# Attention and two MLPs on one core: a product of two weights handed to the scheduler earlier, and a row scaling moved from POOL to ScalarE

## The chip, the cores and the metric

The kernel runs on one core of one Trainium2 chip. The metric is the device time of one execution in microseconds (us). Three runs of the kernel before gave 1234.72, 1235.17 and 1236.8 us; their median is 1235.17 us.

## The reference

Attention over 4 batches of 12 heads, 448 positions, head size 64, feeds two MLPs over the 1792 rows that it makes. All in float32 precision.

```python
q_n, k_n = rmsnorm(q, g_q), rmsnorm(k, g_k)
scores = scale * np.matmul(q_n, k_n.transpose(0, 1, 3, 2))
attn = np.exp(scores - np.max(scores, axis=-1, keepdims=True))
attn = attn / (np.sum(attn, axis=-1, keepdims=True) + 1e-09)
x = np.matmul(attn, v)            # laid out as 1792 x 768
h = x @ w_in                      # 768 -> 2048
x = np.maximum(0.01 * h, h) @ w_out
a, b = x @ w1, x @ w2             # 768 -> 1024 each
out = ((a * b) @ w3) @ w_last     # w_last is moe2_w_out
```

## The kernel before

Every float32 product is made of three matmuls of rounded parts: a tile x is split into `xh` (rounded) and `xl` (the rest), and likewise a weight into `wh` and `wl`; the three are wh·xh, wh·xl and wl·xh (`group`, L491). Since nothing stands between w3 and w_last, the kernel multiplies these two weights with each other first: `combine_weights` (L511) makes w3·w_last, 1024 x 768, in 384 matmuls into the tile `pw`, each 128 x 384, and stores the result in DRAM (`wc`). The two weights arrive as 64-bit words; each piece is loaded (L402), turned into float32 (`to_float32`: POOL L420, ScalarE L422 and L425, VectorE L427 and L431) and split (`split`: ScalarE L456, VectorE L184). The eight pieces of w_last are kept in `lasth` and `lastl` for the whole product, the sixteen of w3 go through `wh` and `wl`.

The attention works on pairs of heads. A pair takes two **slots**, one for each half of its query rows, so that there are 48 slots. A slot's work is: the score matmuls `ps` (L123, 12 of them), the scaling with the row's minimum (VectorE L254), the exponential with its row sum (ScalarE L263), 1 / sum (VectorE L268, L269), and the multiplication of the four 112 x 448 tiles `p` by it (POOL, L272). Two slots later TensorE transposes them (`pt`, L286), VectorE and ScalarE copy the transposes to `pth` (L103, L101), and a matmul with v gives the pair's values (`po`, L123). The preparation of later pairs (square sums L148 and L149, keys L204 to L219) lies between.

Two generators are interleaved in `fill` (L978): the attention's steps, and a stream of MLP matmuls handed out in proportion to the steps done. From slot `COMBINE_SLOTS[0]` to slot `COMBINE_SLOTS[1]` the stream is `combine_weights`; then, up to slot 26, it is the first two of four parts of the first MLP for batch 0 (`early`, its matmuls in the tile `ps_mm`); after slot 26 it is all the rest for batches 0 and 1 (`late`). The parts of the weights that `early` made are kept in DRAM and loaded again by SyncE (SP) for `late` (L443). This order of the program, with the priorities of L43, goes to a scheduler that writes each engine's final order. So a number in `COMBINE_SLOTS` changes the order on every engine. After slot 47 the last two batches run through the MLPs alone.

The lines that matter below are L40 (the two slots), L272 (the multiplication), L978 to L995 (`fill`), L1023 to L1027 (its calls).

Of the kernel before, what the change touches and what calls it, by code (L numbers as in the profile page):

```python
# [11 lines left out]
AF = mybir.ActivationFunctionType  # L12
ALU = mybir.AluOpType
# [23 lines left out]
KEYS_AHEAD = 1  # L37
P_TILES = 8
TOGETHER = 2000
COMBINE_SLOTS = 5, 17  # L40
EARLY = 2
PRIORITY = dict(
    values=200, p_transpose=600, scores=600, prep=600, load=100, statistics=100, keys=50  # L43
# [4 lines left out]
def attention_then_moe(  # L48
# [22 lines left out]
    nc = tc.nc  # L71
# [17 lines left out]
    def bank(name):  # L89
        return psum.tile([P, 512], F32, tag="ps", name=name)  # L90
# [24 lines left out]
    def together(matmuls):  # L115

        one = None
        for out, a, x, begin, end in matmuls:
            with ExitStack() as behind:
                if one is not None:  # L120
                    behind.enter_context(tc.high_priority(TOGETHER))
                    behind.enter_context(tc.issue_after(one.ins))
                one = nc.tensor.matmul(out, a, x, start=begin, stop=end)  # L123
        return one
# [100 lines left out]
    def scores(t, half):  # L225

        if t >= NH // 2:
            return
        x = pairs[t]
        pair = heads[2 * t : 2 * t + 2]  # L230
        if half == 0:
            x["sums"] = small.tile([CP, 2, NCH], F32, tag="sum", name="sum")
            for h in pair:
                h["p"] = [None] * NCH
        ps = [[bank("ps")[:CP, :S] for _ in range(2)] for _ in range(2)]
        chunks = range(2 * half, 2 * half + 2)
        terms = [("qh", "kh"), ("ql", "kh"), ("qh", "kl")]
        x["scored"] = together(
            (
                ps[c % 2][e],  # L240
                x[q][mine(e), c * CP : (c + 1) * CP],
                x[k][mine(e)],
                n == 0,
                n == len(terms) - 1,
            )
            for c in chunks
            for n, (q, k) in enumerate(terms)
            for e in range(2)
        )
        for c in chunks:  # L250
            for e, h in enumerate(pair):
                p = h["p"][c] = att.tile([CP, S], F32, tag="p", name="p", bufs=P_TILES)
                low = small.tile([CP, 1], F32, tag="low", name="low", bufs=8)
                nc.vector.tensor_scalar(  # L254
                    p,
                    ps[c % 2][e],
                    x["scale"][:, e, c : c + 1],
                    None,
                    op0=ALU.mult,
                    op1=ALU.min,  # L260
                    accum_out=low,
                )
                exps[t] = nc.scalar.activation(  # L263
                    p, p, AF.Exp, bias=low, scale=-1.0, accum_out=x["sums"][:, e, c : c + 1]
                )

        r = small.tile([CP, 2, 2], F32, tag="r", name="r")
        nc.vector.tensor_scalar_add(r, x["sums"][:, :, 2 * half : 2 * half + 2], 1e-9)  # L268
        nc.vector.reciprocal(r, r)  # L269
        for c in chunks:  # L270
            for e, h in enumerate(pair):
                nc.gpsimd.tensor_scalar(  # L272
                    h["p"][c], h["p"][c], r[:, e, c % 2 : c % 2 + 1], 1.0, op0=ALU.mult, op1=ALU.mult
                )

    def mine(i):
        return slice(D * (i % 2), D * (i % 2 + 1))
# [64 lines left out]
    def attention_steps():  # L342

        for t in range(NH // 2 + 2):
            ranked(values, t - 2)
            yield 2 * t
            for half in range(2):
                s = 2 * t + half
                for kc in range(NCH):
                    ranked(p_transpose, s - 2, kc)  # L350
                    yield s
                ranked(scores, t, half)
                for _ in range(NCH):
                    yield s
                if half:
                    ranked(keys, t + KEYS_AHEAD)
                    ranked(load, t + 2)
                    ranked(statistics, t + STATS_AHEAD)
                else:
                    load_v(2 * t)  # L360
                    ranked(prep, t + 1)
                    load_rows(t + STATS_AHEAD)
                run_later()
                yield s
# [610 lines left out]
    per_slot = 2 * NCH + 2  # L975
    slots = COMBINE_SLOTS

# [99 lines left out]
```

## Time and profile before

| | |
|---|---|
| median of three runs | 1235.17 us |
| the profiled execution's own time | 1229.4 us |
| its span, first to last instruction | 1227.6 us |
| TensorE (PE) matmuls busy | 1157.6 us, 94% |
| VectorE (DVE) busy | 777.9 us, 63% |
| ScalarE (ACT) busy | 662.7 us, 54% |
| GpSimd (POOL) busy | 390.2 us, 32% |
| mean granted TensorE clock | 0.967 of full |

Busy shares are means over stretches with different limits. The attention with its stream of MLP work takes the first 810 us; in the last 418 us POOL does nothing. A wait is put down to the releaser that came last, and the chain of waits is followed back from the last instruction. "Granted clock" is the share of the full TensorE clock: 1.00 is 2.4 GHz and 0.50 is 1.2 GHz, and a value between is a mean over both.

### The profile page before, as it was taken

The numbers are of one execution on the slowest core, as the hardware profiler recorded it, in microseconds if no ns is written. First come the engines' busy times: TensorE is split into PE (matmuls) and PEld (weight loads), VectorE is DVE, ScalarE is ACT, GpSimd is POOL, SyncE is SP. The second block draws the span as 40 slices with busy tenths as digits, with TensorE's granted clock in tenths as the row PEclk, the third lists the DMA queues.
The fourth block names the chain that finished last, engine by engine and source line by source line (L and its number), as shares of the span: only waits on it lengthen the run. The fifth ranks groups of instructions, "written<-read, shape, count | busy, mean of one in ns | idle before, by whom it ended". The sixth has DMA issues, their size and how long they took to land.

```text
span 1227.6 us, 17006 instructions
## 1 busy us (share of the span) xinstructions
PE 1157.6 (94%) x6096; PEld 966.4 (79%) x6096; DVE 777.9 (63%) x1511; ACT 662.7 (54%) x1343; POOL 390.2 (32%) x474
## 2 busy tenths in 40 slices
PE   2779999998979999999999999999999999899998
PEld 1456778776668788888878888888999999699997
DVE  7997777889852375857854465276346455954553
ACT  7676667777644475666654664245443334533431
POOL 3654345677731344367642443200000000000000
PEclk8669999998889999999999999999999999999999
DMA  8433335877576534534421441062212021112202
GB/s 256 143 99 108 113 123 199 303 257 262 186 298 193 172 119 157 165 126 165 166 88 64 152 161 53 34 227 64 77 35 78 26 77 59 58 39 67 72 35 99
DMA packets 65381, 158.93 MB, mean 129 GB/s; under 512 B 7440, under 2 KB 32784, under 8 KB 65296
## 3 DMA queue, kind: packets, MB, share of 16 engines
q1 hardware_dynamic: 45648, 73.94, 19.0%
q10 hardware_dynamic: 10944, 49.29, 12.0%
q0 software_dynamic: 8704, 34.61, 7.5%
q8 instruction: 48, 0.79, 0.3%
q14 instruction: 37, 0.30, 0.1%
HBM read 114.95 MB, written 42.86 MB: 129 GB/s over the span
## 4 chain that ended last, share of the span: by engine, by line
PE 64%; DVE 7%; DMA 4%; ACT 1%; issue 1%; POOL 1%; SPq 0%; ACTq 0%; DVEq 0%; POOLq 0%
PE ps_mm L499 26%; PE ps_o L499 13%; PE ps_b L499 9%; PE ps_c L499 5%; PE po L123 3%; PE pt L286 3%; PE ps L123 3%; PE ps_a L499 2%; DVE ol L184 1%; DVE wl L184 1%; DMA wh<-kept_first_mlp_h 1%; DMA qk_sb<-qk 1%; DMA x_f<-xd 1%; DMA w<-w_out 1%; DVE acc L863 1%
## 5 line engine op out<-in xcount | busy, mean ns | idle before, releaser
L272 POOL TENSOR_SCALAR p<-p,r 112x448 f32<-112x448 f32 x192 | 150.9, 802 | 63.4 <-DVE r L269 34.4
L184 DVE TENSOR_TENSOR wl<-raw,wh 128x512 fp32r<-128x512 f32 (+1 forms) x136 | 113.9, 839 | 74.9 <-ACT wh L705 35.1
L499 PE MATMUL ps_mm<-xh,wh 128*128 128x448 f32 x384 | 143.0, 373 | 7.3 <-DMA wh<-kept_first_mlp_h 7.0
L263 ACT ACTIVATE p<-p,low 112x448 f32<-112x448 f32 x192 | 126.5, 661 | 40.4 <-DVE p L254 40.1
L499 PE MATMUL ps_mm<-xl,wh 128*128 128x448 f32 x384 | 146.8, 382 | 0.0
L499 PE MATMUL ps_mm<-xh,wl 128*128 128x448 f32 x384 | 141.9, 370 | 0.1
L254 DVE TENSOR_SCALAR_CACHE_REDUCE p<-ps,rs 112x448 f32<-112x448 f32 x192 | 122.0, 678 | 27.7 <-PE ps L123 27.7
L286 PE MATMUL pt<-ident,p 112*112 112x112 f32 x768 | 107.2, 278 | 25.7 <-POOL p L272 20.7
L286 PEld LDWEIGHTS pt<-ident,p 112*112 112x112 f32 x768 | 87.5, 143 | 52.8 <-POOL p L272 26.6
L499 PE MATMUL ps_mm<-gl,wh 128*128 128x448 f32 x288 | 109.5, 380 | 0.0
L427 DVE SCALAR_TENSOR_TENSOR raw<-w,raw 128x768 uint32<-128x768 uint32 (+1 forms) x80 | 76.0, 949 | 51.1 <-ACT w L425 50.9
L499 PE MATMUL ps_mm<-gh,wl 128*128 128x448 f32 x288 | 106.2, 369 | 0.9 <-DMA wl<-kept_first_mlp_l 0.9
L499 PE MATMUL ps_mm<-gh,wh 128*128 128x448 f32 x288 | 106.3, 372 | 0.6 <-DMA wh<-kept_first_mlp_h 0.6
L499 PE MATMUL ps_o<-gl,wh 128*128 128x448 f32 x288 | 104.1, 365 | 0.0
L499 PE MATMUL ps_o<-gh,wl 128*128 128x448 f32 x288 | 100.5, 365 | 0.0
L499 PE MATMUL ps_o<-gh,wh 128*128 128x448 f32 x288 | 99.1, 365 | 0.0
L420 POOL TENSOR_SCALAR raw<-w 128x768 f32<-128x768 f32 (+1 forms) x80 | 70.2, 878 | 84.3 <-DVE wl L184 51.9
L422 ACT ACTIVATE w<-w 128x768 uint32<-128x768 uint32 (+1 forms) x80 | 63.5, 794 | 47.0 <-DMA w<-w_out 16.1
L425 ACT ACTIVATE w<-w 128x768 f32<-128x768 f32 (+1 forms) x80 | 63.1, 789 | 45.6 <-POOL raw L420 45.6
L499 PEld LDWEIGHTS ps_mm<-xh,wh 128*128 128x128 f32 x384 | 73.0, 190 | 15.5 <-DVE y L155 6.3
L123 PE MATMUL po<-pth,v_sb 112*64 112x448 f32 x384 | 80.7, 562 | 1.9 <-ACT pth L101 1.1
L499 PEld LDWEIGHTS ps_mm<-xl,wh 128*128 128x128 f32 x384 | 73.2, 191 | 10.8 <-issue 4.9
(136 smaller groups left out, 2650.8 us busy)
## 6 DMA issues: line engine op xcount, KB each, us to landing
w<-w_in ACTq DMA_DIRECT2D x16, 768.0 KB, 4.8
w<-w_out ACTq DMA_DIRECT2D x24, 512.0 KB, 3.8
w<-w ACTq DMA_DIRECT2D x16, 768.0 KB, 4.5
qk_sb<-qk SPq DMA_DIRECT2D x48, 224.0 KB, 4.2
w<-w3t ACTq DMA_DIRECT2D x16, 512.0 KB, 3.3
kept_first_mlp<-raw POOLq DMA_DIRECT2D x16, 384.0 KB, 4.7
kept_first_mlp<-raw POOLq DMA_DIRECT2D x24, 256.0 KB, 3.5
kept_second_mlp<-raw POOLq DMA_DIRECT2D x16, 384.0 KB, 3.0
```

The costliest lines, as they stand in the source:

```text
L123: one = nc.tensor.matmul(out, a, x, start=begin, stop=end)
L184: e.tensor_tensor(out, x, y.bitcast(F32), op=ALU.subtract)
L254: nc.vector.tensor_scalar(p, ps[c % 2][e], x["scale"][:, e, c : c + 1], None, op0=ALU.mult, op1=ALU.min, accum_out=low,)
L263: exps[t] = nc.scalar.activation(p, p, AF.Exp, bias=low, scale=-1.0, accum_out=x["sums"][:, e, c : c + 1])
L272: nc.gpsimd.tensor_scalar(h["p"][c], h["p"][c], r[:, e, c % 2 : c % 2 + 1], 1.0, op0=ALU.mult, op1=ALU.mult)
L286: nc.tensor.transpose(pt[:, c * CP : (c + 1) * CP], h["p"][c][:, kc * CP : (kc + 1) * CP], ident[:CP, :CP],)
L420: nc.gpsimd.tensor_scalar(out, h, 0.0, 1.0, op0=ALU.mult, op1=ALU.mult)
L422: nc.scalar.activation(low, low, AF.Copy, scale=2.0**-29)
L425: nc.scalar.activation(h, h, AF.Copy, scale=2.0**-112)
L427: nc.vector.scalar_tensor_tensor(top, high, 3, top, op0=ALU.logical_shift_left, op1=ALU.bitwise_or)
L499: nc.tensor.matmul(ps[:, :n], a, x, start=begin, stop=end, skip_group_check=on)
L863: nc.vector.tensor_tensor(acc[m, b], ps[:, :S], acc[m, b], op=ALU.add)
```

## The change

`COMBINE_SLOTS` goes from 5, 17 to 1, 14: the product of w3 and w_last is handed out from slot 1 to slot 14 and no longer from slot 5 to slot 17, and the early part of the first MLP from slot 14 and no longer from slot 17, up to slot 26 as before. And ScalarE multiplies the tiles `p` by 1 / sum, with an activation `Copy` whose scale is a column of `r`; before, POOL did. No operation is added or left out.

```diff
-COMBINE_SLOTS = 5, 17
+COMBINE_SLOTS = 1, 14
...
         for c in chunks:
             for e, h in enumerate(pair):
-                nc.gpsimd.tensor_scalar(
-                    h["p"][c], h["p"][c], r[:, e, c % 2 : c % 2 + 1], 1.0, op0=ALU.mult, op1=ALU.mult
+                nc.scalar.activation(
+                    h["p"][c], h["p"][c], AF.Copy, scale=r[:, e, c % 2 : c % 2 + 1]
                 )
```

The built programs show what the scheduler makes of it, at three places. The first is TensorE between the score matmuls of slot 2 and those of slot 3 (`pt` are the transposes of slots 0 and 1, `pw` the product of the two weights). Before:

```order
L123 MATMUL ps<-kl,qh 112x448 x2
L286 MATMUL pt<-ident,p 112x112 x28
L123 MATMUL ps<-kh,qh 112x448 x2
L123 MATMUL ps<-kh,ql 112x448 x2
L123 MATMUL ps<-kl,qh 112x448 x2
```

With the change:

```order
L123 MATMUL ps<-kl,qh 112x448 x2
L286 MATMUL pt<-ident,p 112x112 x28
L499 MATMUL pw<-lasth,wh 128x384
L499 MATMUL pw<-lastl,wh 128x384
L499 MATMUL pw<-lasth,wl 128x384
```

Twelve `pw` matmuls now stand ahead of slot 3's scores; before, the first `pw` stood behind slot 6's. Counted over the whole order: ahead of the first score matmul of slot 8 there were 31 `pw` and now are 115; ahead of slot 16's there were 289 `pw` and no `ps_mm`, and now are all 384 `pw` and 64 `ps_mm`, with eight `pt` fewer; ahead of slot 28's both orders have the same matmuls, and from there on they are alike.

The second place is ScalarE behind the exponentials of slots 0 and 1 (`w` is a weight on its way to float32, `r` is 1 / sum). Before:

```order
L456 ACTIVATE lasth<-raw 128x768
L402 DMA w_862<-w_last 128x1536
L148 ACTIVATE sq<-qk_sb 112x512
L148 ACTIVATE qk_sb<-qk_sb 112x512
L425 ACTIVATE w_754<-w_754 128x512
L153 ACTIVATE y<-ss 112x16
L456 ACTIVATE lasth<-raw 128x768
```

With the change:

```order
L456 ACTIVATE lasth<-raw 128x768
L402 DMA w_487<-w_last 128x1536
L148 ACTIVATE qk_sb<-qk_sb 112x512
L272 ACTIVATE p<-p,r 112x448 x4
L148 ACTIVATE sq<-qk_sb 112x512
L456 ACTIVATE lasth<-raw 128x768
L402 DMA w_534<-w_last 128x1536
L422 ACTIVATE w_487<-w_487 128x768
L153 ACTIVATE y<-ss 112x16
L272 ACTIVATE p<-p,r 112x448 x4
L456 ACTIVATE wh<-raw 128x512
```

The eight multiplications of slots 0 and 1 now stand among the conversions of w_last. Ahead of ScalarE's first exponential of slot 8 there are now 32 multiplications, four more pieces of w3 (twelve activations of 128 x 512) and five more copies of `pw` (L534) than before; between there and slot 16's another 32 multiplications, and ten more activations of weights and one copy of `pw` fewer than before.

The third place is SP where `late` begins, at slot 26: the loads of the kept weight parts. Before:

```order
L443 DMA wh<-kept_first_mlp_0_h 128x768
L167 DMA qt_sb<-qt 128x448
L178 DMA v_sb<-v 112x2x256
L443 DMA wh<-kept_first_mlp_1_h 128x768
L443 DMA wl<-kept_first_mlp_0_l 128x768
L443 DMA wl<-kept_first_mlp_1_l 128x768
```

With the change:

```order
L443 DMA wh<-kept_first_mlp_0_h 128x768
L443 DMA wl<-kept_first_mlp_0_l 128x768
L178 DMA v_sb<-v 112x2x256
L134 DMA qk_sb<-qk 112x2x256 x2
L167 DMA qt_sb<-qt 128x448
L443 DMA wh<-kept_first_mlp_1_h 128x768
L443 DMA wl<-kept_first_mlp_1_l 128x768
```

On TensorE the same place, with the tiles' numbers (3960 and 3961 are the parts of weight 0, 3970 is one of weight 1), read before:

```order
L286 MATMUL pt_4010<-ident_81,p_3853 112x112
L499 MATMUL ps_mm_3982<-xl_2218,wh_3960 128x448
L499 MATMUL ps_mm_4025<-xh_2217,wh_3970 128x448
L286 MATMUL pt_4037<-ident_81,p_3693 112x112
L286 MATMUL pt_4037<-ident_81,p_3701 112x112
```

and now reads:

```order
L286 MATMUL pt_4010<-ident_81,p_3734 112x112
L499 MATMUL ps_mm_3982<-xl_2503,wh_3960 128x448
L499 MATMUL ps_mm_3982<-xh_2502,wl_3961 128x448
L499 MATMUL ps_mm_3982<-xh_2502,wh_3960 128x448
L499 MATMUL ps_mm_3982<-xl_2503,wh_3960 128x448
```

Before, the first matmul that needs weight 1 stood third, ahead of the transposes, of slot 26's scores and of nearly all the products of weight 0; now 18 products of weight 0 come ahead of it, and both parts of weight 0 are loaded ahead of weight 1.

## Rows read from the trace of the kernel before

**Rows 1.** Busy time by stretches cut at slots 0, 8, 16, 28: engines' busy, clock, DMA.

```profile
core 0: us, PE busy (x) PEld busy (x) DVE busy (x) ACT busy (x) POOL busy (x), PEclk, DMA share, GB/s
14.00:104.00 90.00, 63.36 (x300) 40.63 (x300) 78.40 (x173) 67.11 (x146) 50.18 (x50) 0.72 0.44 141
104.00:199.00 95.00, 93.53 (x567) 71.27 (x566) 75.34 (x178) 67.12 (x159) 43.91 (x58) 1.00 0.40 128
199.00:290.00 91.00, 89.92 (x506) 68.84 (x506) 74.63 (x138) 66.26 (x139) 62.52 (x85) 1.00 0.78 273
290.00:360.00 70.00, 56.52 (x287) 42.49 (x286) 57.38 (x115) 43.31 (x96) 42.16 (x59) 0.83 0.68 252
...
399.00:810.00 411.00, 407.50 (x2264) 341.10 (x2263) 240.04 (x477) 231.00 (x472) 177.41 (x202) 1.00 0.38 127
```

**Rows 2.** Waits of PE over the span: total us, times, longest.

```profile
PE pt L286 <- POOL p L272: 20.7, 8, 10.4
...
PE ps_mm L499 <- DMA wh<-kept_first_mlp_h: 7.6, 3, 6.1
```

**Rows 3.** PE's timeline, matmuls of pw: start us, us.

```profile
90.48 0.52 PE L499 MATMUL pw<-lastl,wh 128*128 128x384 f32 x1
90.80 0.52 PE L499 MATMUL pw<-lasth,wl 128*128 128x384 f32 x1
...
101.22 0.34 PE L499 MATMUL pw<-lasth,wh 128*128 128x384 f32 x1
101.39 0.34 PE L499 MATMUL pw<-lastl,wh 128*128 128x384 f32 x1
```

**Rows 4.** The chain that ended last: start us, us, what.

```profile
707.37 7.49 PE ps_mm L499 x36
...
790.60 1.53 PE pt L286 x16
```

**Rows 5.** ACT's timeline, an exponential and the reading of its sum.

```profile
22.97 0.66 ACT L263 ACTIVATE p<-p,low 112x448 f32<-112x448 f32 x1
23.53 0.19 ACT L263 ACTIVATION_READ_ACCUMULATOR p<-p,low 112x1 f32 x1
```

**Rows 6.** ACT by form, 14 to 104 us: busy us, mean ns, idle before.

```profile
L422 ACT ACTIVATE w<-w 128x512 uint32<-128x512 uint32 x7 | 4.7, 668 | 0.1
L425 ACT ACTIVATE w<-w 128x512 f32<-128x512 f32 x6 | 4.1, 677 | 2.1 <-POOL raw L420 2.1
...
L456 ACT ACTIVATE wh<-raw 128x512 fp32r<-128x512 f32 x4 | 2.5, 620 | 0.0
```

**Rows 7.** ACT by form, 0 to 350 us.

```profile
L534 ACT ACTIVATE wo<-pw 128x384 f32<-128x384 f32 x16 | 7.6, 478 | 2.8 <-PE pw L499 2.8
```

**Rows 8.** Waits of ACT, 14 to 104 us, the two longest.

```profile
ACT w L425 <- POOL raw L420: 6.2, 4, 4.1
ACT sq L148 <- DMA qk_sb<-qk: 6.2, 2, 3.6
```

**Rows 9.** Timelines of DVE and POOL, 19 to 38 us.

```profile
19.26 0.94 DVE L427 SCALAR_TENSOR_TENSOR raw<-w,raw 128x768 uint32<-128x768 uint32 x1
...
30.32 1.28 DVE L427 SCALAR_TENSOR_TENSOR raw<-w,raw 128x768 uint32<-128x768 uint32 x1
...
37.51 1.15 DVE L150 TENSOR_SCALAR ss<-ss 112x16 f32<-112x16 f32 x1
...
30.14 8.49 POOL L272 TENSOR_SCALAR p<-p,r 112x448 f32<-112x448 f32 x8
```

**Rows 10.** PE's timeline where `late` begins.

```profile
345.91 0.45 PE L499 MATMUL ps_mm<-xl,wh 128*128 128x448 f32 x1
352.43 0.71 PE L499 MATMUL ps_mm<-xh,wh 128*128 128x448 f32 x1 [6.08 <-DMA wh<-kept_first_mlp_h]
```

**Rows 11.** SP's timeline of DMA issues at the same place.

```profile
340.95 0.33 SPq L443 DMA_DIRECT2D wh<-kept_first_mlp_h  x1
...
345.38 0.82 SPq L443 DMA_DIRECT2D wl<-kept_first_mlp_l  x2
```

**Rows 12.** Busy time in a stretch ahead of the first pw.

```profile
80.00:90.00 10.00, 9.13 (x41) 6.14 (x39) 9.61 (x25) 4.89 (x13) 6.49 (x7) 0.50 0.01 3
```

## Prediction

> **What bounds the kernel now.** I cut the span where slots 0, 8, 16 and 28 begin on PE and read each stretch for the engine that is never free. From 399 us on PE is busy 407.5 of 411 us at the full clock [rows 1], and the orders are alike from there: nothing can be won. So the question is when slot 28 begins, at 399 us before. From 104 to 290 us PE is full too, 93.5 of 95 and 89.9 of 91 us. PE time is lost in two places. In 14 to 104 us PE is busy 63.4 of 90 us at a mean clock of 0.72 (a mix of 1.2 and 2.4 GHz), which is at most 63.4 x 0.72 = 46 us of work at full speed; DVE is busy 78.4 there, so it is nearly full, ACT 67.1, POOL 50.2. The longest wait that PE has for another compute engine is here, 20.7 us in eight pieces for the multiplication on POOL [rows 2]. In 290 to 360 us PE is busy 56.5 of 70 us at 0.83, about 47 us of work: 23 us are lost, 6.1 of them in one wait for a kept weight [rows 2, 10].
>
> **The change, term by term**, each as a shift of the beginning of slot 28.
>
> *PE work moved forward.* Ahead of slot 8 there are 84 more `pw`. At the full clock they start 0.17 us apart [rows 3]: 84 x 0.175 = 14.7 us. Ahead of slot 16 it is 95 `pw` (16.6 us), 64 `ps_mm` at 7.49 / 36 = 0.208 us (13.3 us), less eight transposes at 1.53 / 16 = 0.1 us (0.8 us) [rows 3, 4]: 29.1 us. So slots 0 to 7 get 14.7 us of PE work more, slots 8 to 15 get 14.4 more, and slots 16 to 27 get 29.1 less.
>
> *Slots 0 to 7.* What does this cost where PE had room? No row shows the new activation. From below it can cost what an exponential of the same tile occupies, since the exponential does a pointer operand and more: it starts 0.56 us before the reading of its sum [rows 5]; from above its whole 0.66 us. I take 0.56, because ACT's instructions overlap like these two. ACT gets 32 of them, 17.9 us; four pieces of w3, 4 x (0.668 + 0.677 + 0.620) = 7.9 us, less about 0.1 us overlap each, 6.7; five copies of `pw`, 5 x 0.38 = 1.9 [rows 6, 7]. That is 26.5 us on an engine that was busy 67.1 of 90: 93.6 us, 3.6 more than the stretch has. DVE gets thirteen operations of the w3 pieces, at two thirds of the 0.94 us of 128 x 768 [rows 9] 8 us: 86.6 of 90, also nearly full. So ACT becomes the bound. At best it never waits, and slot 8 begins 3.6 us later; at worst it keeps all its 22.9 us of idle time, and slot 8 begins 26.5 us later. Some waits go with the multiplication on POOL (6.2 us were for POOL's part of a conversion), some do not (6.2 us for `qk_sb` to land) [rows 8]. I let 5.4 us stay, nearer to the low end because the scheduler put other ready work between: **+9 us**.
>
> A row bears on DVE's side. The same 128 x 768 operation took 0.94 us with POOL idle and 1.28 us beside POOL's eight multiplications (8.49 us from 30.14), and a 112 x 16 operation took 1.15 us there [rows 9]. The multiplications leave POOL, so DVE should get some of this back: 0.34 us of the first and at most the whole of the second, 1.5 us for two slots and 6 us for eight. The Trainium skill, GPSIMD Engine Reference, section Specifications, says that POOL's SBUF interfaces are shared with VectorE, with contention for DVE's two-port modes and two-input instructions; the trace agrees. By that sentence all of it would come back, and the term would be nearer +5 than +9; I keep +9, since ACT and not DVE is last here.
>
> *Slots 8 to 15.* PE was full and stays so: 93.5 + 14.4 = 108 us at the least, **+14.4**. ACT: 67.1, 17.9 for 32 multiplications and about 7 for ten weight activations (between 6 and 9, by their columns from rows 6) come to 92 of 109 us, which fits.
>
> *Slots 16 to 27.* PE has **-29.1**. ACT: 66.3 + 43.3 in the 161 us up to 360 [rows 1], 48 x 0.56 = 27 more, less the 16 that went forward (8.6 and 7): 121 us, which fits.
>
> *The loss around 290 to 360 us.* Before, PE stopped for 6.08 us at weight 1 [rows 10], whose load was issued at 340.95, before `wl` of weight 0, at 345.38 [rows 11]. Now 18 products of weight 0 (18 x 0.208 = 3.7 us) stand ahead of weight 1, and both parts of weight 0 are loaded first; the half clock behind the stop goes too. Against this, weight 1 now stands behind a load of `qk_sb` on SP. The ends are nothing (the stall finds another place) and 23 us (all of the loss). I take **-8**: this stop and 2 us of its half clock. The rest hangs on loads of 64-bit weights that are now spread over more slots, which I do not count.
>
> *From slot 28 on.* ACT gets 80 x 0.56 = 45 us: 231 + 45 = 276 of 411 us. PE covers it. What it costs if a copy out of PSUM comes late behind a multiplication: between 0 and 10 us; **+2**.
>
> Sum: 9 + 14.4 - 29.1 - 8 + 2 = **-11.7 us**. Against the profiled execution's 1229.4 us that is 1217.7; that execution is 5.8 us under the median of the runs, so on the median's scale I forecast **1223 us**.
>
> **Rivals.**
>
> *ACT's queue holds everything up (slower).* ACT works in order, and a multiplication waits for `r` from DVE; behind it stand exponentials, conversions and copies out of PSUM that PE waits for. If ACT keeps all its idle time in slots 0 to 7, the first term is +26.5: 26.5 + 14.4 - 29.1 - 8 + 2 = +6, 1241 us. If it keeps it in slots 8 to 15 too (27.9 us, so 120 where PE needs 109) it is another 11: 1252. It decides from 17 of 22.9 us kept, where the sum passes zero. For it: both ACT and DVE are then full, and their waits are on each other. Against: eight places where PE waited for POOL are gone.
>
> *The early product wakes the clock and the later loss goes (faster).* In 80 to 90 us PE was busy 9.13 of 10 at the 1.2 GHz level [rows 12]; `pw` starts 0.32 us apart at 90 us and 0.17 at 101 us, after eleven microseconds of nearly unbroken matmuls [rows 3]. With `pw` from slot 3 on, PE is denser sooner. If ACT also waits for nothing (+3.6) and the loss at 290 to 360 us goes altogether (-23): 3.6 + 14.4 - 29.1 - 23 + 2 = -32, 1203; half of that way, -22, 1213. The Trainium skill, TensorE: Matmul & The Clock Gate, Part 1, says that the clock is throttled by default and that activity releases it; the trace has both levels as it says. Without such a release the 84 `pw` cost 84 x 0.32 = 27 us of PE in slots 0 to 7, which with 63.4 makes 90 of 99 us and still fits, so that the clock alone does not decide.
>
> *The loads set the pace (no change).* From 199 to 360 us the DMA engines are busy 0.78 and 0.68 of the time at 273 and 252 GB/s [rows 1]. If slot 28 waits for the kept weights and not for PE, the work moved forward only makes room to wait in: 1235 us. Against it: PE was full up to 290 us under the same load.
>
> That the change does not do what it says is not among them: the order shows both parts.
>
> **How the numbers follow.** Less than 0.2% (2.5 us) is about what a measurement of this kernel cannot tell from no change. The forecast, between -4 and -18 us: 0.45. The faster rival, beyond -18: 0.21. The loads: 0.12. The slower rival, from +3: 0.22. So faster 0.66, same 0.12, slower 0.22. For eight in ten I leave out half of what lies beyond -30 and what lies beyond +8, a tenth each: 1206 to 1243 us. The likeliest case by itself is 1217 to 1231.
>
> **What would show it.** In the profile of the changed kernel: slot 8's first score matmul at about 113 us and slot 16's at about 222 (before 104 and 199), yet slot 28's at about 385; ACT busy over 90 of the 99 us of slots 0 to 7; no wait of `pt` for POOL, and short ones for ACT in its place; no stop of 6 us at the first kept weights; PE still over 99% busy after slot 28. I am wrong if slot 8 begins after 125 us (the queue of ACT), if a loss of 20 us stays between slots 16 and 28 (the loads), or if PE's idle time after slot 28 grows by more than 10 us.

## The result, and the profile after

The changed kernel takes 1217.32 us (median of four runs, 1213.81 to 1222.62) against 1235.38 us (1234.72 to 1236.8) for the kernel before in the same comparison. The ratio is 0.9856, with a 95% interval of 0.9828 to 0.9884: 17.8 us or 1.4% faster. The forecast was 1223 us, the range 1206 to 1243. The profiled execution took 1215.56 us, with a span of 1213.8 us and a mean granted clock of 0.975 (before 1229.4, 1227.6 and 0.967). So the two profiles are 13.8 us apart and not 17.8: the kernel before was profiled in an execution 6 us under its median, the change in one 1.8 us under its own, and some 4 us of the gain stand in none of the stages below.

First the busy time of the engines in stretches cut where slots 0, 8, 16, 22 and 28 now begin, with one more cut at 343 us. The columns are those of [rows 1].

```profile
14.00:115.00 101.00, 72.23 (x380) 51.43 (x380) 82.76 (x182) 89.93 (x190) 26.53 (x25) 0.80 0.50 156
115.00:227.00 112.00, 108.56 (x639) 86.41 (x638) 82.19 (x181) 92.95 (x204) 36.41 (x49) 0.97 0.56 184
227.00:294.00 67.00, 63.27 (x357) 44.86 (x357) 59.35 (x128) 63.72 (x143) 31.37 (x46) 0.97 0.79 273
294.00:343.00 49.00, 47.81 (x280) 34.70 (x280) 44.20 (x99) 46.25 (x102) 19.35 (x27) 1.00 0.69 248
343.00:382.00 39.00, 39.00 (x219) 32.86 (x216) 12.51 (x38) 21.88 (x50) 5.57 (x5) 1.00 0.63 202
382.00:794.00 412.00, 410.21 (x2266) 343.39 (x2266) 235.20 (x477) 274.52 (x552) 115.19 (x122) 1.00 0.38 127
```

Slot 28 begins at 382 us where it began at 399. Slots 0 to 7 and 8 to 15 have become longer, 101 and 112 us against 90 and 95. The gain is the third to fifth row together: 155 us where slots 16 to 27 took 200. From 294 us on PE has hardly a gap and the full clock, where in 290 to 360 us before it was busy 56.5 of 70 us at 0.83 [rows 1].

The same in one table for the two kernels and five of the runs below. A stage begins with the first score matmul of its first slot on PE. A cell has the length of the stage in us, then in brackets what PE lost in it: the time in which no matmul ran, and half of the busy time in stretches at the 1.2 GHz level.

| kernel | slots 0 to 7 | 8 to 15 | 16 to 21 | 22 to 27 | 28 to the end |
|---|---|---|---|---|---|
| before | 89.2 (26.0, 18.6) | 95.0 (1.5, 0) | 86.0 (0.9, 0) | 114.0 (13.6, 8.1) | 828.8 (14.3, 1.7) |
| the change | 100.4 (28.4, 13.2) | 111.9 (3.4, 3.4) | 67.6 (3.7, 1.7) | 88.1 (1.2, 0) | 831.4 (13.5, 5.1) |
| e1, slots alone | 96.4 (27.9, 9.3) | 106.3 (0.9, 0) | 73.3 (9.3, 1.7) | 92.0 (2.0, 0) | 836.3 (16.7, 8.1) |
| e2, ScalarE alone | 91.6 (31.7, 12.8) | 95.0 (1.4, 1.7) | 86.7 (2.2, 1.7) | 105.8 (9.9, 4.6) | 830.9 (15.3, 1.7) |
| e10, POOL's time put back | 102.6 (32.0, 10.9) | 105.8 (0, 0) | 73.6 (8.9, 3.7) | 97.7 (5.2, 5.1) | 835.3 (16.9, 5.0) |
| e14, from slot 0 | 100.6 (23.1, 6.5) | 100.2 (0, 0) | 66.4 (4.3, 0) | 93.9 (3.1, 3.3) | 834.1 (15.1, 6.5) |
| e15, POOL's time, no wait | 120.4 (38.8, 20.1) | 114.7 (4.7, 1.7) | 68.0 (2.9, 3.4) | 91.5 (2.0, 3.4) | 834.1 (16.7, 4.0) |

What is left of a stage when its losses are taken off is PE's work at full speed. It went from 44.6 to 58.8 us in slots 0 to 7, from 93.5 to 105.1 in slots 8 to 15, and from 85.1 + 92.3 to 62.2 + 86.9 in slots 16 to 27: 25.8 us forward by the first two, 28.3 by the last. The last column differs by some us between profiles of kernels with one order there (before 828.8, e6 832.3), so 2 or 3 us in it say nothing. A row is one execution: e1's, 1219.86 us, is the fastest of its six (median 1225.71), so its row shows e1 some 6 us too short.

The waits of PE after, total us, times, longest:

```profile
PE pt L286 <- ACT p L272: 18.5, 4, 14.7
PE pk L209 <- DVE y L155: 12.6, 1, 12.6
...
PE ps_mm L499 <- DMA wl<-kept_first_mlp_l: 1.1, 1, 1.1
...
PE ps_mm L499 <- DMA wh<-kept_first_mlp_h: 0.6, 1, 0.6
```

The wait of the transposes for the multiplication has changed its releaser, and its total little (20.7 us for POOL [rows 2]); its longest piece has grown from 10.4 to 14.7 us. The wait for kept weights has gone from 7.6 us for `wh` [rows 2] and 0.9 for `wl` to 1.7 for both parts. SP's timeline where `late` begins (start us, us, DMA issue):

```profile
327.20 0.35 SPq L443 DMA_DIRECT2D wh<-kept_first_mlp_h  x1
328.38 0.34 SPq L443 DMA_DIRECT2D wl<-kept_first_mlp_l  x1
332.05 0.33 SPq L178 DMA_DIRECT2D v_sb<-v  x1
332.48 0.97 SPq L134 DMA_DIRECT2D qk_sb<-qk  x2
335.34 0.35 SPq L167 DMA_DIRECT2D qt_sb<-qt  x1
335.86 0.35 SPq L443 DMA_DIRECT2D wh<-kept_first_mlp_h  x1
```

Both parts of weight 0 are asked for by 328.4 us, 14 us ahead of slot 26 (342.7). The `wh` of weight 1, issued at 340.95 before [rows 11], goes out at 335.86.

What the multiplication costs on ACT: its group over the span (busy us, mean ns, idle before), (192 of them, 113 us in all):

```profile
L272 ACT ACTIVATE p<-p,r 112x448 f32<-112x448 f32 x192 | 113.0, 672 | 11.1 <-DVE r L269 10.8
```

And a piece of ACT's timeline (start us, us):

```profile
33.54 1.85 ACT L272 ACTIVATE p<-p,r 112x448 f32<-112x448 f32 x3
35.02 0.33 ACTq L402 DMA_DIRECT2D w<-w_last  x1
35.22 0.73 ACT L272 ACTIVATE p<-p,r 112x448 f32<-112x448 f32 x1
```

One lasts 0.67 us, and three of them take (35.22 - 33.54) / 3 = 0.56 us of ACT each, the price that the prediction took from an exponential [rows 5].

### The profile page after: what moved, and what is told of

Its sections match the earlier page's. It is cut to its first block, busy times and chain, and to the rows that moved or that the text cites. A ratio compares the mean times of both kernels' runs of the same rounds, so it can differ in the third digit from the quotient of the medians.

```text
span 1213.8 us, 16887 instructions
## 1 busy us (share of the span) xinstructions
PE 1150.1 (95%) x6096; PEld 964.3 (79%) x6096; DVE 759.7 (63%) x1511; ACT 761.7 (63%) x1535; POOL 238.2 (20%) x282
## 4 chain that ended last, share of the span: by engine, by line
PE 63%; ACT 13%; DVE 8%; DMA 7%; issue 4%; POOL 1%; ACTq 0%; SPq 0%; DVEq 0%; POOLq 0%
PE ps_mm L499 24%; PE ps_o L499 13%; PE ps_b L499 9%; PE ps_c L499 5%; ACT p L272 3%; PE po L123 3%; PE pt L286 3%; ACT p L263 3%; PE ps L123 3%; PE ps_a L499 2%; DMA w<-w_out 2%; ACT w L425 1%; DVE ol L184 1%; DMA w<-w_in 1%; DMA w<-w3t 1%
## 5 line engine op out<-in xcount | busy, mean ns | idle before, releaser
L286 PE MATMUL pt<-ident,p 112*112 112x112 f32 x768 | 100.7, 266 | 26.2 <-ACT p L272 18.5
L286 PEld LDWEIGHTS pt<-ident,p 112*112 112x112 f32 x768 | 82.6, 135 | 51.3 <-ACT p L272 21.1
L272 ACT ACTIVATE p<-p,r 112x448 f32<-112x448 f32 x192 | 113.0, 672 | 11.1 <-DVE r L269 10.8
L427 DVE SCALAR_TENSOR_TENSOR raw<-w,raw 128x768 uint32<-128x768 uint32 (+1 forms) x80 | 69.2, 867 | 55.8 <-ACT w L425 55.4
L420 POOL TENSOR_SCALAR raw<-w 128x768 f32<-128x768 f32 (+1 forms) x80 | 69.5, 869 | 166.5 <-DVE wl L184 105.8
L499 PE MATMUL ps_o<-gh,wl 128*128 128x448 f32 x288 | 100.6, 366 | 0.0
L705 ACT ACTIVATE wh<-raw 128x512 fp32r<-128x512 f32 (+1 forms) x52 | 36.3, 698 | 77.3 <-PE ps_b L499 34.5
L456 ACT ACTIVATE wh<-raw 128x512 fp32r<-128x512 f32 (+1 forms) x84 | 59.8, 714 | 33.4 <-PE ps_mm L499 33.4
```

What stands on the lines that cost most here:

```text
L272: nc.scalar.activation(h["p"][c], h["p"][c], AF.Copy, scale=r[:, e, c % 2 : c % 2 + 1])
L286: nc.tensor.transpose(pt[:, c * CP : (c + 1) * CP], h["p"][c][:, kc * CP : (kc + 1) * CP], ident[:CP, :CP],)
L420: nc.gpsimd.tensor_scalar(out, h, 0.0, 1.0, op0=ALU.mult, op1=ALU.mult)
L427: nc.vector.scalar_tensor_tensor(top, high, 3, top, op0=ALU.logical_shift_left, op1=ALU.bitwise_or)
L456: self.rounded = nc.scalar.activation(flat[0], x, AF.Copy)
L499: nc.tensor.matmul(ps[:, :n], a, x, start=begin, stop=end, skip_group_check=on)
```

## The experiments

Each has the change or the kernel before as its base. Times are medians, ratios are to the kernel before on the same chip with their 95% intervals.

**e1: the slots alone.** The kernel before with the new slots; POOL multiplies.

```diff
-COMBINE_SLOTS = 5, 17
+COMBINE_SLOTS = 1, 14
```

> Only the slots change (1, 14); POOL still multiplies. Theory A (PE work moved forward pays, ACT's extra work costs): the same work stands ahead as in the change (115 pw ahead of slot 8, 384 pw and 55 ps_mm ahead of slot 16), without ACT's 18 us in slots 0 to 7, so the gain is like that of the change or larger: 1210 to 1222 us. Theory B (the multiplication's move carries the gain, since p is ready sooner and DVE is free of POOL): within 4 us of before, 1231 to 1239, and slot 28 begins near 399 us.

Measured: 1225.71 us (1219.86 to 1228.88), ratio 0.9903 (0.9876 to 0.9929).

**e2: the multiplication alone.** The change with the old slots.

```diff
-COMBINE_SLOTS = 1, 14
+COMBINE_SLOTS = 5, 17
```

> Only the multiplication moves to ScalarE; the slots stay at 5, 17. Theory A: 13 pw more stand ahead of slot 8 and 10 ahead of slot 16, ACT gets 18 us more in slots 0 to 7, slot 28 begins within 6 us of 399 and the time is 1230 to 1240 us. Theory B: 1213 to 1225 us, and slot 8 begins before 104 us.

Measured: 1228.2 us (1224.83 to 1231.63), ratio 0.9931 (0.9906 to 0.9956). Both times lie between what the two theories expected: each part gains by itself, 1.0% and 0.7%, and together they give 1.4%, somewhat less than the sum. So the multiplication on ScalarE is, over the whole kernel, no price paid for the slots. It gains some 8 us where the prediction gave it only costs. In e2 slot 8 begins at 105.6 us, 1.8 later than before, so none of that is gained ahead of slot 8. By the table, e1's loss is smaller than that of the kernel before in slots 22 to 27 (2.0 us for 21.7) and larger in 16 to 21 (11.0 for 0.9); e2 keeps most of the loss in 22 to 27 (14.5).

**e3 and e4: one end of the slots each**, in the change.

```diff
-COMBINE_SLOTS = 1, 14
+COMBINE_SLOTS = 1, 17
```

> The changed kernel with the slots 1, 17: the product begins early, the first MLP late as before (89 pw ahead of slot 8, 309 ahead of slot 16, no ps_mm there). Theory A (work moved into PE's idle time of slots 0 to 7 pays): most of the slots' gain is here, 1218 to 1223 us. Theory C (the earlier start of the first MLP pays, since its weights are loaded and converted earlier and PE's loss in slots 22 to 27 goes): no gain over the multiplication alone, 1226 to 1232 us, with 10 us or more lost in slots 22 to 27.

```diff
-COMBINE_SLOTS = 1, 14
+COMBINE_SLOTS = 5, 14
```

> The changed kernel with the slots 5, 14: the product begins late as before, the first MLP early (39 pw ahead of slot 8, all 384 and 64 ps_mm ahead of slot 16). Theory A: little over the multiplication alone, 1224 to 1231 us. Theory C: as good as the change, 1213 to 1220 us, with under 5 us lost in slots 22 to 27.

Measured: 1219.06 us (1215.7 to 1222.26), ratio 0.9881 (0.9856 to 0.9905), and 1220.5 us (1216.99 to 1225.92), 0.9892 (0.9864 to 0.992). Against e2's 0.9931 either end alone brings most of what the two bring together (0.9856); the intervals of the two ends overlap, so which end does more is not told apart. In slots 22 to 27, measured as in the table, e3 loses 8.1 us (6.4 idle, 1.7 at the half clock) and e4 1.1, so it is the earlier start of the first MLP that goes with a small loss there.

**e5: ScalarE loaded further.** In the change, 32 more activations in slots 0 to 7, into a tile that nobody reads.

```diff
+                if t < 4:
+                    spare = small.tile([CP, 300], F32, tag="spare", name="spare", bufs=1)
+                    nc.scalar.activation(
+                        spare, h["p"][c][:, :300], AF.Copy, scale=r[:, e, c % 2 : c % 2 + 1]
+                    )
```

> The changed kernel with 32 activations more in slots 0 to 7, each 300 columns of p into a tile that nobody reads: about 0.44 us each, 14 us of ACT. Theory A (ACT is last in slots 0 to 7): slot 8 begins 8 to 14 us later than in the change and the time is 8 to 14 us above it, 1225 to 1232. If ACT has room there: within 4 us of the change.

Measured: 1214.98 us (1212.24 to 1218.48), ratio 0.9822 (0.9797 to 0.9846). The window from 14 to 115 us of that run, columns as above:

```profile
14.00:115.00 101.00, 72.07 (x395) 53.39 (x395) 85.87 (x185) 99.98 (x216) 25.98 (x26) 0.83 0.51 161
```

ACT is busy 99.98 us where the change has 89.93, and slot 8 begins at 115.1 instead of 114.7. Ten microseconds more on ACT cost nothing there: ACT does not set the length of slots 0 to 7. (The extra work also moved the scheduler's order, 135 `pw` instead of 115 ahead of slot 8, so the test is of ACT's room, not of an unchanged order.)

**e6 and e7: the order of the kept loads alone**, in the kernel before. In e6 all the loads at L443 follow one another in order of use; in e7 only the load of `v` goes behind the first weight's second part.

```diff
-                    nc.sync.dma_start(y, part)
+                    with tc.issue_after(start["kept"].ins) if "kept" in start else ExitStack():
+                        start["kept"] = nc.sync.dma_start(y, part)
```

> The kernel before, with the loads of the kept weight parts chained in the order of their use: both parts of weight 0 ahead of weight 1; up to slot 24 its order of PE has the same matmuls as before. If the stop of 6.1 us at weight 1 was a matter of order: no such stop, and 5 to 9 us less than before, 1226 to 1230. If the loads set the pace: the stop shows up at another kept weight and the time is within 3 us of before.

```diff
-        nc.sync.dma_start(x, v[b, j : j + 2].rearrange("h p n d -> p h n d"))
+        kept = start.get("kept")
+        with tc.issue_after(kept.ins) if kept else ExitStack():
+            nc.sync.dma_start(x, v[b, j : j + 2].rearrange("h p n d -> p h n d"))
...
+                if "kept" not in start:
+                    start["kept"] = one
```

> The kernel before with one load moved on SP: at the beginning of late, the load of v for the fourteenth pair comes behind the first kept weights (wh 0, qt, wh 1, wl 0, v, and no longer wh 0, qt, v, wh 1, wl 0). If the stop of 6 us is SP standing in front of that v, whose buffer is not free, with the kept weights queued behind: the stop falls to under 3 us, slot 28 begins 4 to 9 us earlier, 1226 to 1231. If the weights' own buffers or the DMA engines hold it: the stop stays near 6 us and the time is within 3 us of before.

Measured: 1235.16 us, ratio 0.9996 (0.9974 to 1.0017), and 1232.43 us (1229.2 to 1235.9), 0.9977 (0.9962 to 0.9993). PE's stop at the kept weights stays (idle time before the matmul and its releaser in brackets). On PE's timeline of e6:

```profile
353.09 0.74 PE L500 MATMUL ps_mm<-xh,wl 128*128 128x448 f32 x1 [5.94 <-DMA wl<-kept_first_mlp_l]
```

On PE's timeline of e7:

```profile
353.57 0.71 PE L503 MATMUL ps_mm<-xh,wh 128*128 128x448 f32 x1 [4.89 <-DMA wh<-kept_first_mlp_h]
```

And on PE's timeline of e2, with the old slots:

```profile
347.00 0.71 PE L499 MATMUL ps_mm<-xh,wh 128*128 128x448 f32 x1 [6.17 <-DMA wh<-kept_first_mlp_h]
```

So the order on SP alone is worth 0 to 3 us, and does not make the stop. It goes with the end of the product: in the kernels that end it at slot 17 PE's longest wait for a kept weight is 6.1 us (before), 5.9 (e6), 4.9 (e7), 6.2 (e2) and 2.4 (e3); in the nine that end it at slot 14 it is at most 1.8. What differs there is when the early part's last parts are stored and how long transfers take. Transfers issued in 318 to 365 us, before (KB of one, median us from issue to landing):

```profile
kept_first_mlp_h<-wh POOLq DMA_DIRECT2D x4, 256.0 KB, 2.5
...
qt_sb<-qt SPq DMA_DIRECT2D x1, 224.0 KB, 12.3
v_sb<-v SPq DMA_DIRECT2D x1, 224.0 KB, 11.3
```

And in the change:

```profile
kept_first_mlp_h<-wh POOLq DMA_DIRECT2D x2, 256.0 KB, 5.0
...
qt_sb<-qt SPq DMA_DIRECT2D x2, 224.0 KB, 4.7
v_sb<-v SPq DMA_DIRECT2D x1, 224.0 KB, 4.9
```

Before, four such stores fall in that stretch and the loads behind them on SP take 11 and 12 us; now two do, and the loads of `qt` and `v` take 5. That the stores slow the loads is not shown: no run tried it by itself, and the loads of `qk_sb` in the same stretch go the other way (3.7 us before, 5.3 in the change).

**e8 and e9: where the multiplication's gain lies.** In the change, POOL multiplies for the first four pairs only (e8), or for all but these (e9).

```diff
+                if t < 4:
+                    nc.gpsimd.tensor_scalar(
+                        h["p"][c], h["p"][c], r[:, e, c % 2 : c % 2 + 1], 1.0, op0=ALU.mult, op1=ALU.mult
+                    )
+                    continue
```

> The changed kernel with POOL multiplying for the first four pairs (slots 0 to 7) and ScalarE for the rest. If the multiplication's part of the gain (8 us between the slots alone and the change) comes from p being ready sooner at the start: as the slots alone, 1223 to 1228. If it comes from POOL being free later, where it also converts and stores weights: as the change, 1214 to 1219.

> The opposite: ScalarE multiplies for the first four pairs, POOL for the rest. If the gain comes from the start: 1214 to 1219. If it comes from POOL being free later: 1223 to 1228.

(e9 has the same edit with `t >= 4`.) Measured: e8 1216.88 us (1213.03 to 1221.06), ratio 0.9866 (0.9839 to 0.9894); e9 1222.33 us (1220.68 to 1224.13), 0.9906 (0.9881 to 0.9931). e8 cannot be told from the change, e9 not from the slots alone. The gain of the multiplication comes from the pairs after the fourth, that is after slot 7.

**e10: POOL's time put back.** In the change, two small scalings per tile on POOL, into a tile that nobody reads: 384 of them, waiting for `r` as the multiplication did.

```diff
+                for _ in range(2):
+                    spare = small.tile([CP, P], F32, tag="spare", name="spare", bufs=1)
+                    nc.gpsimd.tensor_scalar(
+                        spare, ident[:CP], r[:, e, c % 2 : c % 2 + 1], 1.0, op0=ALU.mult, op1=ALU.mult
+                    )
```

> The changed kernel, and POOL does for each tile p two multiplications of 112 x 128 into a tile that nobody reads, when 1 / sum is there: some 100 us of POOL put back, with no one waiting for its results. If the multiplication's part of the gain is POOL's time (its conversions and stores come sooner, DVE is not slowed): most of 8 us is lost again, 1222 to 1229. If it is the way of p itself (it no longer stands in POOL's queue): as the change, 1214 to 1220.

Measured: 1231.39 us (1225.03 to 1235.43), ratio 0.9962 (0.9946 to 0.9979), above both expectations. PE waits for none of these results, and yet 14 us of the 17.8 are gone, more than the multiplication's own 8. The spare work is also more than what was taken off: it lasts 192 us on POOL, where the 192 multiplications lasted 151 (the group at L272 in the kernel before). So POOL's time alone, without any way of `p` through POOL, costs at least what the multiplication's move gained. Two things can carry it to PE: VectorE beside POOL, and work that stands behind a waiting instruction in POOL's list. Busy time of the engines over the span (share of it, instructions), first of the kernel before:

```profile
PE 1157.6 (94%) x6096; PEld 966.4 (79%) x6096; DVE 777.9 (63%) x1511; ACT 662.7 (54%) x1343; POOL 390.2 (32%) x474
```

The same of the change:

```profile
PE 1150.1 (95%) x6096; PEld 964.3 (79%) x6096; DVE 759.7 (63%) x1511; ACT 761.7 (63%) x1535; POOL 238.2 (20%) x282
```

Of e1, where POOL multiplies:

```profile
PE 1148.4 (94%) x6096; PEld 961.0 (79%) x6096; DVE 778.0 (64%) x1511; ACT 662.2 (54%) x1343; POOL 391.6 (32%) x474
```

And of e10:

```profile
PE 1153.0 (94%) x6096; PEld 964.3 (78%) x6096; DVE 774.8 (63%) x1511; ACT 763.7 (62%) x1535; POOL 430.2 (35%) x666
```

The same 1511 VectorE instructions take 778 us where POOL multiplies, 760 where it does not, and 775 with the spare work. Between the kernel before and the change, 15.6 of the 18.2 us lie in VectorE's part of the weight conversion (`raw<-w,raw`, 160 operations, 154.2 and 138.6 us). One of its operations in slots 16 to 27 (busy us, mean ns), first of e1:

```profile
L431 DVE CUSTOM_DVE_ANT_0 raw<-w,raw 128x1024 uint16<-128x1024 uint16 x9 | 12.0, 1336 | 0.0
```

And of the change:

```profile
L431 DVE CUSTOM_DVE_ANT_0 raw<-w,raw 128x1024 uint16<-128x1024 uint16 x9 | 6.4, 725 | 0.0
```

It reaches PE. PE's longest wait for VectorE in these slots (total us, times, longest), in e1:

```profile
PE ps L123 <- DVE p L254: 3.7, 2, 2.4
```

And in the change:

```profile
PE ps L123 <- DVE p L254: 1.1, 2, 0.6
```

For slots 16 to 27 as a whole, in us (each kernel has 32 of these conversions there, of the same shapes):

| kernel | POOL beside VectorE | POOL busy | the 32 conversions | PE's waits for VectorE | PE's waits for the multiplication |
|---|---|---|---|---|---|
| the change | no multiplication | 56.3 | 26.8 | 1.1 | 0.3 |
| e8 | no multiplication | 58.5 | 28.1 | 0.9 | 4.4 |
| e1 | multiplies | 97.8 | 34.9 | 6.1 | 1.1 |
| e9 | multiplies | 101.5 | 38.1 | 6.5 | 5.1 |
| e10 | spare work | 109.9 | 33.4 | 6.4 | 2.2 |

With POOL loaded, VectorE's conversions last 5 to 11 us longer and PE waits 5 us longer for VectorE, whether POOL multiplies or does work that nobody reads. (Three more kernels in which POOL does not multiply, e4, e5 and e14, have 1.5 to 2.1 us of waits for VectorE there. With the product ending at slot 17 the picture is less clear: 5.9 before, 4.7 in e2, 2.0 in e3.) The waits for `p` itself do not go by the engine that multiplies: 0.3 to 4.4 us for ScalarE, 1.1 to 5.1 for POOL.

The second thing is POOL's list of work, in the order that the scheduler wrote: while POOL waits for `r`, the conversions and stores behind would stand too. Its longest wait for `r` in e10 (total us, times, longest), over the span:

```profile
POOL spare L277 <- DVE r L269: 56.0, 21, 13.9
```

From 223 to 394 us, where slots 16 to 27 lie:

```profile
POOL spare L277 <- DVE r L269: 4.7, 2, 3.4
```

And from 394 us on:

```profile
POOL spare L277 <- DVE r L269: 42.8, 13, 13.9
```

Most of this waiting lies behind slot 27; where e10 loses its time, in slots 16 to 27, it is 4.7 us in two pieces. That speaks for VectorE as the way, and against the waiting.

**e15: the same work without the wait.** As e10, with the constant 1 in place of `r`.

```diff
-                        spare, ident[:CP], r[:, e, c % 2 : c % 2 + 1], 1.0, op0=ALU.mult, op1=ALU.mult
+                        spare, ident[:CP], 1.0, 1.0, op0=ALU.mult, op1=ALU.mult
```

> The change with the same 384 unread scalings of 112x128 on POOL as in the run before (some 100 us of POOL time), but by the constant 1 and not by r, so that POOL waits for nothing ahead of them; the scheduler puts them in gaps of POOL's queue. The run with the scale r took 1231.4 us against 1217.3 for the change. Theory A (what costs there is POOL's time or its use of SBUF beside VectorE): 1227 to 1235 us here too, with slots 16 to 27 losing some 20 us again. Theory B (what costs is that POOL, in order, stands and waits for r while conversions and stores wait behind it; in the profile of that run POOL's longest waits are for r, 56 us in 21 pieces): 1214 to 1221 us, with 5 to 10 us lost in slots 16 to 27. Between them, 1221 to 1227, both count.

Measured: 1244.62 us (1239.53 to 1246.39), ratio 1.0066 (1.0045 to 1.0087), outside both expectations. Free of `r`, the work was put into the first 271 us, and it delayed slots 0 to 7, which took 20 us more than in the change. POOL is nearly full there, as the window of 14 to 115 us has it (26.53 us in the change):

```profile
14.00:115.00 101.00, 61.91 (x276) 42.02 (x276) 74.64 (x152) 74.42 (x154) 89.73 (x174) 0.70 0.42 133
```

And ACT waits for POOL's part of the weight conversions, in 14 to 134 us 24.9 us in ten pieces (total us, times, longest), where the change has 0.8 us in one up to 115 us:

```profile
ACT w L430 <- POOL raw L425: 24.9, 10, 5.6
```

That shows that POOL's time costs where POOL is nearly full, without any wait for `r`. Of slots 16 to 27 only the first 22 us have spare work left (from 249.4 to 271.2 us), and the loss there is 11.7 us, nearer to the change's 6.6 than to e10's 22.9. Since the work moved away from slots 16 to 27, the run does not test there what it was made for. How much of e10's 14 us is VectorE beside POOL and how much is work standing behind POOL's waits is not measured by a run of its own; the waits and conversions above speak for the first.

**e14: the product from the first slot on.** The change with one more slot at the early end.

```diff
-COMBINE_SLOTS = 1, 14
+COMBINE_SLOTS = 0, 14
```

> The changed kernel with the slots 0, 14: 161 pw ahead of slot 8 (115 in the change). If work put into slots 0 to 7 is paid for there by a higher clock alone: slot 8 begins some 6 us later, slot 16 as in the change, and the time is within 3 us of the change, 1214 to 1220. If PE's idle time there can be filled: 3 to 8 us below the change.

Measured: 1210.88 us (1208.64 to 1211.2), ratio 0.9801 (0.9781 to 0.982): faster than both kernels, 6.4 us below the change, as the second expectation had it. Its first two stages:

```profile
14.00:115.00 101.00, 77.73 (x434) 57.02 (x434) 87.87 (x192) 94.77 (x200) 25.88 (x29) 0.86 0.53 164
115.00:215.00 100.00, 100.00 (x585) 75.60 (x584) 75.52 (x171) 86.92 (x190) 36.02 (x46) 1.00 0.57 194
```

There are 161 `pw` ahead of slot 8 instead of 115, and slots 0 to 7 are no longer than in the change (100.6 and 100.4 us). By the table, PE does 71.0 us of full-speed work in them where the change does 58.8: it waits 5.3 us less and loses 6.7 us less to the half clock. Its first `pw` starts at 42.0 us, with 16.9 us of PE's idle time ahead of it and 6.3 behind it up to slot 8; in the change it starts at 45.4, with 17.7 ahead and 10.8 behind. What e14 fills lies behind the first `pw`. PE's room in slots 0 to 7 was not used up by the change.

## Why the prediction was right, and where it was not

The time came inside the range, and the gain of 17.8 us lies at the far end of the forecast's own case (4 to 18 us). The sum came near by luck in part: two of its larger terms were off by 8 and 2.5 us in opposite directions, the first one hit its size for a wrong reason, and the last is no larger than what two profiles differ by there anyway. The shifts are those of the profiled executions, by the table.

| term | predicted | measured |
|---|---|---|
| slots 0 to 7 | +9 | +11.2 |
| slots 8 to 15 | +14.4 | +16.9 |
| slots 16 to 27: work | -29.1 | -28.3 |
| slots 16 to 27: loss | -8 | 22.6 to 6.6, -16.0 |
| from slot 28 | +2 | +2.6 |
| sum | -11.7 | -13.6 |

**Slots 0 to 7: size nearly right, by luck; the reason wrong.** The step that failed is "So ACT becomes the bound". ACT was busy 89.93 of 101 us, and e5 put 10 us more on it at no cost. The stretch is longer because PE got 14.2 us of work more (44.6 to 58.8; the 84 `pw` were reckoned at 14.7) while its idle time stayed, 26.0 and 28.4 us; 5.4 us less were lost to the half clock: 14.2 + 2.4 - 5.4 = 11.2. The kernel before had all its 26.0 us of idle time ahead of its first `pw` (90.0 us). In the change 17.7 us still lie ahead of the first `pw` (45.4 us), and 14.7 of them in one piece up to 34.3 us, when no `pw` could run: the first piece of w3 is split at 40.17. On ACT's timeline:

```profile
40.17 0.69 ACT L456 ACTIVATE wh<-raw 128x512 fp32r<-128x512 f32 x1
```

On PE's:

```profile
45.44 0.67 PE L499 MATMUL pw<-lasth,wh 128*128 128x384 f32 x1
```

The other 10.8 us lie behind it. The 14.7 us, on PE's timeline of the change, stand ahead of the first transposes, those of slot 0:

```profile
34.32 1.00 PE L286 MATMUL pt<-ident,p 112*112 112x112 f32 x4 [14.69 <-ACT p L272]
```

In this one place it is ACT's list of work that holds PE: `r` was there at 29.6 us, ACT was busy without a break from 19.9 us with conversions, exponentials and the preparation of later pairs, and it came to the multiplication at 33.54, where POOL had begun it at 30.14 [rows 9].

"Ahead of slot 8 there are 84 more `pw`" was a good count, then, but the question "what does this cost where PE had room" was put to the wrong engine for the stage as a whole: most of PE's room lay ahead of the first `pw`.

**Slots 8 to 15: size nearly right.** PE had 11.6 us more work, where 14.4 were reckoned, and it was not quite full: 1.9 us more idle time and 3.4 at the half clock, which the prediction did not have, make the 16.9.

**Slots 16 to 27, the work: right**, 28.3 for 29.1 us.

**The loss in 290 to 360 us: the mechanism in part, half the size.** The prediction took -8 between 0 and -23; in slots 22 to 27 the loss fell by 20.5 us (21.7 to 1.2), of which slots 16 to 21 gave 4.5 back (0.9 to 5.4). The stop at weight 1 did go, with its half clock: 7.0 us of waits for kept weights and 3.1 us at the half clock behind them (348.4 to 358.6 us), 10.1 where the term had 8. That it went because "both parts of weight 0 are loaded first" is not shown: e6 and e7 changed that order and kept a stop of 4.9 to 5.9 us. What goes with it in the runs is the end of the product at slot 14; why, stays open.

The mis-sized step is "which I do not count": the rest of the loss, put down to loads of 64-bit weights and taken as nothing. It was 11.6 us before, of which 10.4 went. PE's waits in slots 22 to 27 of the kernel before (total us, times, longest) name no such load themselves:

```profile
PE ps_mm L499 <- DMA wh<-kept_first_mlp_h: 7.0, 2, 6.1
PE ps L123 <- DVE p L254: 2.4, 1, 2.4
PE pt L286 <- DVE pth L103: 2.1, 1, 2.1
PE ps L123 <- ACT pth L101: 1.5, 1, 1.5
PE ps L123 <- DVE xl L184: 0.5, 1, 0.5
```

6.5 us are waits for steps of the attention on VectorE and ScalarE, and 5.0 us are two stretches at the half clock near them. But ScalarE waited for such loads, 9.5 us in 285 to 399 us (total us, times, longest), and in 294 to 382 us of the change for none:

```profile
ACT w L422 <- DMA w<-w_in: 6.4, 3, 3.3
ACT w L422 <- DMA w<-w_out: 3.1, 1, 3.1
```

So the loads may stand behind it, as the prediction supposed; what share is theirs is not shown, and leaving the term at nothing was what mis-sized the loss. e1 has only 2.0 us of loss left in 22 to 27, but 11.0 in 16 to 21, where the change has 5.4.

**The multiplication: a term with the wrong sign.** The prediction counted ACT's time for it and kept "+9, since ACT and not DVE is last here". Ahead of slot 8 it does cost 0 to 4 us (100.4 us against e1's 96.4, 91.6 in e2 against 89.2 before, 100.8 in both e8 and e9), but alone it gains some 8 us over the kernel (e2), after slot 7 (e8, e9), through POOL's time (e10) and, as PE's waits have it, by way of VectorE. The row that pointed there was in the prediction: the VectorE operation of 0.94 us that took 1.28 beside POOL [rows 9]. The Trainium skill, GPSIMD Engine Reference, section Specifications, tells of the shared SBUF interfaces; the traces agree, with 18.2 us of VectorE's busy time less over the span for the same instructions. The prediction weighed this for slots 0 to 7 only, at most 6 us, where in fact nothing was gained (e8); it had no term for it where POOL was busiest, 62.5 of 91 us in 199 to 290 us [rows 1].

**The rivals.** ACT's queue did not hold everything up, the first transposes aside: its waits ahead of slot 8 are short (total us, times, longest).

```profile
ACT w L422 <- DMA w<-w3t: 4.5, 3, 2.2
ACT p L263 <- DVE p L254: 3.3, 4, 2.1
...
ACT p L272 <- DVE r L269: 1.0, 1, 1.0
```

The loads do not set the pace: with the DMA engines as busy as before (0.79 of the time and 273 GB/s in 227 to 294 us, 0.78 and 273 in 199 to 290 before [rows 1]), slot 28 came 16.4 us sooner. The faster rival is the nearest miss: the later loss went by 16 of its 23 us and 5.4 us less were lost to the half clock in slots 0 to 7, but PE's waits at the start stayed, and with them the stage's length. (Its reading of the clock was late: on PE's timeline of the kernel before, `pw` start 0.18 us apart from 92.4 us on, not only at 101.) e14, another kernel, 24.4 us under the kernel before, lies in its range.

**The signs named in advance.** Slot 8 at 114.7 (113 forecast), slot 16 at 226.6 (222), slot 28 at 382.3 (385); no stop at the first kept weights; PE busy 410.2 of 412 us after slot 28. ACT's busy time missed its mark by a hair (89.93 of 101 us, forecast over 90 of 99), and "short ones for ACT" failed in one place, the 14.69 us above.

## What to carry to other kernels

When work is moved forward into an engine's idle time, look first at where in the stretch the idle time lies and whether the moved work is ready by then: a mean share of 63 in 90 us says nothing of that. An operation taken off an engine that is nowhere the bound can still gain, by the engine that it slows: look at the other engine's durations with and without it, and at who waits for that engine. A test that puts unread work back on the relieved engine shows that its time matters, if the work is of the same size and stays in the same place: here it was 192 us for 151 in one run and moved to the start in the other. Where one step of a tuned number helps, try the next: from slot 0 instead of slot 1 was worth another half per cent.

## What the runs showed of the hardware

A scaling of a 112 x 448 tile by a column takes 0.67 us on ScalarE, issued every 0.56 us, and 0.80 us on the mean on POOL (192 in 150.9 us), 0.64 in the median. On POOL a scaling of 112 x 128 took 376 ns in the median with a column of `r` as its factor (e10) and 298 ns with a constant (e15). VectorE's 128 x 768 integer operation at L427 took 1092 ns on the mean before and 1024 ns in the change, in forty instances each, with the multiplications gone from POOL and the order moved. Its 128 x 1024 operation at L431 took 883 ns in e1 and 719 in the change, which have the same slots, and 875 before and 713 in e2, which have the old ones, forty instances each: with POOL's multiplications some 160 ns more.
